# The last 64 keys' scores: from one matmul over a padded block to one matmul per head on half the array

## The chip, the cores and the metric

The kernel runs on one core of a Trainium2 chip. The core has five engines with a queue each, and each works through its own instructions in order: PE (TensorE: matmuls and transposes, which write PSUM), ACT (ScalarE), DVE (VectorE), POOL (GpSimd) and SP, which here only starts DMAs. They wait for each other through semaphores. PSUM has eight banks of 512 float32 columns by 128 partitions. The metric is the device time of one execution in microseconds (us), as the median of several.

## The reference

What is computed, cut to what matters (8 batches, 8 heads, 576 positions, 64 numbers per head; the FFN is 512 to 1024 to 512 wide):

```python
scores = scale * np.matmul(q, k.transpose(0, 1, 3, 2))
kth = np.partition(scores, -top_k, axis=-1)[..., -top_k:-top_k + 1]   # top_k = 32
scores = np.where(scores >= kth, scores, -1000000000.0)
attn = np.exp(scores - np.max(scores, axis=-1, keepdims=True))
attn = attn / (np.sum(attn, axis=-1, keepdims=True) + 1e-09)
attn_out = np.matmul(attn, v)
...
h = np.maximum(x @ w_in, 0.0)             # x: attn_out, heads side by side
conv_out = sum(conv_w[j] * h shifted by j - 1 along the sequence, j = 0, 1, 2)
gate = 1.0 / (1.0 + np.exp(-conv_out))
out = (h * gate) @ w_out
```

## The kernel before

**Tiles.** Two heads make a head pair: head 0 lies on partitions 0 to 63 of the tiles q and k, head 1 on partitions 64 to 127, so that each head's contraction over 64 numbers uses one half of the array's rows. The 576 queries are four blocks of 128 and one of 64. A tile of work is 128 query rows of one head by 576 keys; a block of 128 queries gives two tiles (h = 0 and h = 1, called a pair here), and the block of 64 gives a single one, with the two heads on the two halves of the partitions. There are 128 pairs and 32 singles, 288 tiles in all.

**One tile's way.** Its 576 scores come as 512 "main" keys, one PSUM bank for each head (`s_ps`, L242), and 64 "edge" keys. Head 0's edge is keys 512 to 575. Head 1's keys are stored rotated, so that its edge is its first 64 columns. ACT copies the scores to a row buffer `rows` in SBUF (eight of them, L248 for the main part, L256 for the edges of both heads in one instruction, L250 for a single). DVE finds the 32nd largest by MAX8 over pieces (L266, L286, L288, L315, L319), ACT makes signs (L300, `sides`) and exponentials (L312), POOL multiplies by the signs (L305), DVE masks (L333, tile `e`). PE transposes the 512 main columns of `e` into the bank `pt` (L345), and once a pair the two edges into `mixed` (L358, `tails`); ACT copies them out (L353, L363); PE multiplies with v (L377, L380, into `mixed`) and ACT copies the result out (L387, `xt`). Sums are transposed into a score bank now and then (L398, `norms`).

**The edges before.** The host adds 128 columns to k: head 0's last 64 keys on partitions 0 to 63 in the first 64 columns, head 1's on partitions 64 to 127 in the last 64, and zeros elsewhere. One matmul over all 128 rows of the array (L225, `edge_product`) then gives both heads' edges side by side in 128 columns of the bank `mixed`.

**The FFN.** It runs beside the attention of later batches: 12 matmuls make one unit of the first product in the bank `me` (L454, `e_mm` in the code), ACT applies ReLU to it (L468), POOL and DVE do the convolution and the gate, ACT the tanh (L515), and 12 or 24 further matmuls in the bank `mc` make a block of the output (L611), which ACT copies out (L627).

**Order.** PE, ACT, DVE and POOL run in the order in which `iteration(it)` is written; nothing reorders them. Iteration `it` issues work for nine tiles at different stages, each on its engine: scores of tile it+3, their copy to `rows` for tile it+2, and so on, down to transposes of tile it-5. Within an iteration PE does: the four transposes of tile it-5; FFN matmuls as far as a budget allows (`run_units`); `norms`; `tails`; the edge product of the next pair, if the next tile starts one; the scores, if this tile starts a pair (or is a single); the products with v. ACT does: ReLU and output copies of finished FFN units, `sides`, the copy of a tile's main scores and (for h = 0) of the pair's edges, the copy of `pt`, the copy of the transposed edges (`tailed`), the copies `xt` (`av_out`), the exponentials, tanh. So iterations alternate: in one, PE computes a pair's scores; in the next, ACT copies head 0's scores and the edges, and PE does `tails`, and before the change also the next pair's edge product. A tile in PSUM is waited for as a whole: a matmul into `mixed` waits until ACT has read what an earlier instruction wrote there, in other columns too.

Of the kernel before, what the change touches and what calls it, by code (L numbers as in the profile page):

```python
# [69 lines left out]
def attend_and_feed(ctx: ExitStack, tc: tile.TileContext, q, k, v, weights, out, shared, finish=None):  # L70
# [61 lines left out]
    edge_ps, tail_ps, x_ps = mixed[:, 0:P], mixed[:, P:2 * P], [mixed[:, i * P:(i + 1) * P] for i in (2, 3)]  # L132
    flat = rows.rearrange("p a c -> p (a c)")
# [87 lines left out]
    def edge_product(t):  # L221
        t.edged = True
        row = row_of(t.st.i)
        at = slice(row, row + P)
        nc.tensor.matmul(edge_ps, lhsT=t.pc.nat["q"][:, at], rhs=t.pc.nat["k"][:, S:S + 2 * TAIL], start=True, stop=True)  # L225

    def scores(t):
# [3 lines left out]
        if t.single:  # L231
            for to, n, ps_of in ((0, MAIN, s_ps[0]), (MAIN, TAIL, edge_ps)):
                for h, d in enumerate(rows_of):
                    at = (to + TAIL * h) % S
                    nc.tensor.matmul(ps_of[rows_of[1 - h], 0:n], lhsT=qx[d, row:row + TAIL], rhs=kx[d, at:at + n],  # L235
                                     start=True, stop=True)
        elif t.h == 0:
            at = slice(row, row + P)
            if not t.edged:
                edge_product(t)  # L240
            for h, d in enumerate(rows_of):
                nc.tensor.matmul(s_ps[h], lhsT=qx[d, at], rhs=kx[d, h * TAIL:h * TAIL + MAIN], start=True, stop=True)  # L242

    def evacuate(t):
        t.row = rows[:, t.n % XBUFS]
        x = t.x = t.row[:, 8:S + 8]
        at = TAIL if t.h else 0
        nc.scalar.copy(out=x[:, at:at + MAIN], in_=s_ps[t.h])  # L248
        if t.single:
            nc.scalar.copy(out=x[:, MAIN:S], in_=edge_ps[:, 0:TAIL])  # L250
        elif t.h == 0:
            r = t.n % XBUFS
            if r + 1 < XBUFS:
                first, step = r * (S + 16) + 8 + MAIN, S + 16 - MAIN
                ends = flat[:, first:first + 2 * step].rearrange("p (h c) -> p h c", h=2)[:, :, 0:TAIL]
                nc.scalar.copy(out=ends, in_=edge_ps.rearrange("p (h c) -> p h c", h=2))  # L256
            else:
                nc.scalar.copy(out=x[:, MAIN:S], in_=edge_ps[:, 0:TAIL])
                nc.scalar.copy(out=rows[:, 0, 8:8 + TAIL], in_=edge_ps[:, TAIL:2 * TAIL])
# [422 lines left out]
    for b in range(B):  # L682
        for part, blocks in enumerate(PARTS):
            for g in range(NPAIR):
# [5 lines left out]
                for i in blocks:  # L690
# [4 lines left out]
                    for h in range(1 if single else 2):  # L695
                        t = Box()
                        t.n, t.k, t.h, t.pc, t.st, t.single = len(work), pc.n, h, pc, st, single
                        t.ends, t.edged = single or h == 1, False
# [28 lines left out]
    def run_units(budget, only=None):  # L727
        while budget > 0.0 or (only is not None and only.cur is not None):
            for lane in lanes if only is None else (only,):
# [52 lines left out]
    def iteration(it):  # L782
# [5 lines left out]

        for lane in lanes:
            while lane.finished and lane.finished[0].room():  # L790
                lane.waiting -= 1
                lane.finished.popleft().emit()
# [18 lines left out]
        if tE is not None:  # L811
            transposed(tE)
# [3 lines left out]
        for st in outs:  # L816
            av_out(st)
            if st.final and st.pc.g % 2:
                norm_wait.append((it + NORM_LAG, st.pc))

# [57 lines left out]
        if n + 1 < NT and not (work[n].single or work[n + 1].single or work[n + 1].h):  # L878
            edge_product(work[n + 1])
# [33 lines left out]
    if finish is not None:  # L913
        finish(edge_ps[0:1, 0:1])
# [70 lines left out]
def _layout(inputs):  # L985
# [12 lines left out]
    ends = np.zeros((B, H // 2, 2, D, 2, S - main), k.dtype)  # L998
    for h in range(2):
        ends[:, :, h, :, h] = k[:, h::2, main:].transpose(0, 1, 3, 2)  # L1000
    ends = ends.reshape(B, H // 2, 2 * D, -1)
    tails = np.zeros((B, H // 2, 2, S - main, 2, D), v.dtype)
    for h in range(2):
# [4 lines left out]
        "k": np.concatenate([pairs(k, lambda h: h % 2 == 1), ends], axis=-1),  # L1008
# [30 lines left out]
```

## Time and profile before

| | |
|---|---|
| Median of 3 runs | 1125.31 us (1123.97 to 1125.52) |
| The profiled execution's own time | 1126.22 us |
| Its span (first to last instruction) | 1124.3 us |
| Busy: PE, DVE, ACT, POOL | 1041.0 (93%), 1044.5 (93%), 985.1 (88%), 959.8 (85%) us |
| Chain that ended last | PE 72%, DVE 17%, ACT 8%, DMA 1% |
| Idle of PE ahead of L358 (128 and 32 instructions) | 31.3 and 12.2 us |
| Idle of PE ahead of L225 (256 records of 128 matmuls) | 13.0 us |

A float32 matmul stands in the trace as two passes, each with its own load of weights (LDWEIGHTS, shown as PEld); the counts of L225 and L242 are twice the number of matmuls for that reason. Durations of one instruction overlap with the next one's on every engine, so the distance between two starts says what an instruction takes from its engine. The first 225 us hold the conversion of the FFN's weights and a batch without FFN work; after the last tile, at about 1060 us, only FFN work is left.

### The profile page before, as it was taken

To read this page: it belongs to the slowest core of one execution; us is meant where nothing else is said; L and a number is where in the kernel's file an instruction comes from. 1 tells how busy PE (TensorE), PEld (TensorE's weight loads), DVE (VectorE), ACT (ScalarE), POOL (GpSimd) and SP (SyncE) were. 2 spreads that over 40 slices of the span, in tenths; PEclk is the share of its full clock that TensorE was granted. 3 is DMA by queue.
4 is the path that set the end of the run, shared out by engine and by line. 5 is a ranking of instruction groups with operands and counts; after the bars stand their busy time and mean duration, and the time that the engine had idled before them with its cause. 6 is when DMAs were issued, how large, how long until landed. Compare 5 with 4: busy or idle time off the path is not lost.

```text
span 1124.3 us, 28000 instructions
## 1 busy us (share of the span) xinstructions
PE 1041.0 (93%) x7970; PEld 766.5 (68%) x7970; DVE 1044.5 (93%) x5822; ACT 985.1 (88%) x2504; POOL 959.8 (85%) x1260
## 2 busy tenths in 40 slices
PE   6765589999999999999999999999999999999997
PEld 1443356676777777776777777776777777776885
DVE  6999999999999999999999999999999999999760
ACT  6999989999899998989989898989989898989641
POOL 5989979799898989899898999899898999899800
PEclk9989889999999999999999999999999999999999
DMA  7232231123221331223221321223221331222101
GB/s 254 89 101 79 68 100 56 61 75 115 74 78 51 119 100 54 71 74 123 73 71 60 119 99 54 70 74 126 70 74 60 115 97 60 69 72 82 27 27 44
DMA packets 71157, 92.28 MB, mean 82 GB/s; under 512 B 12848, under 2 KB 37712, under 8 KB 70992
## 3 DMA queue, kind: packets, MB, share of 16 engines
q1 hardware_dynamic: 70992, 90.38, 25.1%
q8 instruction: 66, 1.08, 0.4%
q14 instruction: 99, 0.81, 0.2%
HBM read 80.76 MB, written 9.58 MB: 80 GB/s over the span
## 4 chain that ended last, share of the span: by engine, by line
PE 72%; DVE 17%; ACT 8%; issue 1%; DMA 1%; SPq 0%; ACTq 0%
PE mc L611 15%; PE me L454 14%; PE pt L345 11%; PE mixed L377 11%; PE s L242 9%; DVE cand L266 4%; DVE e L333 3%; DVE z L315 3%; PE mixed L380 2%; PE s L235 2%; PE mixed L225 2%; ACT weights_ps L312 2%; PE mixed L358 2%; PE weights_ps L611 1%; ACT side L300 1%
## 5 line engine op out<-in xcount | busy, mean ns | idle before, releaser
L266 DVE MAX8 cand<-rows 128x8 f32<-128x82 f32 (+1 forms) x2016 | 483.9, 242 | 0.0
L305 POOL TENSOR_TENSOR z<-rows,side 128x579 f32<-128x579 f32 x288 | 347.3, 1206 | 58.5 <-ACT side L300 56.2
L333 DVE SCALAR_TENSOR_TENSOR e<-rows,kth,weights_ps 128x576 f32<-128x576 f32 x288 | 232.2, 806 | 1.5 <-PE mixed L358 0.9
L454 PE MATMUL me<-x_hi,wi 128*128 128x258 f32 (+1 forms) x952 | 229.9, 312 | 1.0 <-ACT g L468 1.0
L312 ACT ACTIVATE weights_ps<-rows,z 128x576 f32<-128x576 f32 x288 | 219.9, 764 | 6.1 <-DVE e L333 4.4
L300 ACT ACTIVATE side<-rows 128x576 bf16<-128x576 f32 x288 | 222.9, 774 | 0.0
L315 DVE MAX8 z<-z 128x8 f32<-128x576 f32 x288 | 214.3, 744 | 1.8 <-POOL z L305 1.8
L345 PEld LDWEIGHTS pt<-ident,e 128*128 128x128 f32 x1152 | 124.5, 144 | 121.5 <-issue 47.6
L611 PE MATMUL mc<-wo,split 128*128 128x512 f32 x732 | 197.1, 402 | 0.0
L353 ACT COPY pT<-pt 128x512 f32<-128x512 f32 x256 | 152.5, 596 | 49.0 <-PE pt L345 48.0
L345 PE MATMUL pt<-ident,e 128*128 128x128 f32 x1152 | 193.6, 292 | 0.2 <-DVE e L333 0.2
L242 PE MATMUL s<-k,q 64*128 64x512 f32 x512 | 178.3, 671 | 3.7 <-ACT rows L248 3.6
L248 ACT COPY rows<-s 128x512 f32<-128x512 f32 x288 | 166.6, 578 | 16.2 <-PE s L242 13.2
L377 PE MATMUL mixed<-pT,vn 128*64 128x128 f32 (+1 forms) x2560 | 166.1, 273 | 2.1 <-ACT pTt L363 2.1
L454 PEld LDWEIGHTS me<-x_hi,wi 128*128 128x128 f32 x952 | 162.9, 191 | 1.7 <-ACT g L468 1.7
L377 PEld LDWEIGHTS mixed<-pT,vn 128*64 128x64 f32 x2560 | 130.7, 139 | 24.1 <-issue 7.2
L611 PEld LDWEIGHTS mc<-wo,split 128*128 128x128 f32 x732 | 128.9, 189 | 20.5 <-issue 0.2
L454 PE MATMUL me<-x_lo,wi 128*128 128x258 f32 (+1 forms) x476 | 142.0, 298 | 0.0
L487 POOL TENSOR_SCALAR t<-g,cr 128x256 f32<-128x256 f32 (+1 forms) x230 | 117.4, 511 | 0.0
L286 DVE MAX8 rows<-cand 128x8 f32<-128x21 f32 x576 | 107.0, 186 | 0.0
L501 POOL TENSOR_TENSOR t<-t,t 128x256 f32<-128x256 f32 (+1 forms) x115 | 92.3, 803 | 9.6
L454 PEld LDWEIGHTS me<-x_lo,wi 128*128 128x128 f32 x476 | 91.1, 191 | 0.0
(133 smaller groups left out, 1788.0 us busy)
## 6 DMA issues: line engine op xcount, KB each, us to landing
k<-in_k_dram SPq DMA_DIRECT2D x64, 352.0 KB
q<-in_q_dram SPq DMA_DIRECT2D x64, 288.0 KB
vn<-in_v_main_dram SPq DMA_DIRECT2D x64, 256.0 KB
out_dram<-o SPq DMA_DIRECT2D x26, 256.0 KB
rb<-row SPq DMA_DIRECT2D x64, 96.0 KB
raw<-in_w_in_dram SPq DMA_DIRECT2D x16, 256.0 KB
vt<-in_v_tail_dram SPq DMA_DIRECT2D x64, 64.0 KB
raw<-in_w_out_dram SPq DMA_DIRECT2D x16, 256.0 KB
```

Of the source, the lines that this page charges most:

```text
L242: nc.tensor.matmul(s_ps[h], lhsT=qx[d, at], rhs=kx[d, h * TAIL:h * TAIL + MAIN], start=True, stop=True)
L248: nc.scalar.copy(out=x[:, at:at + MAIN], in_=s_ps[t.h])
L266: yield lambda c=c, at=at, n=n: nc.vector.max(out=t.cand[:, c:8 * CHUNKS:CHUNKS], in_=t.x[:, at:at + n])
L300: nc.scalar.activation(out=t.side[:, 2:S + 2], in_=t.x, func=AF.Sign, scale=-OVER, bias=t.row[:, 7:8], accum_out=t.cnt)
L305: nc.gpsimd.tensor_tensor(t.z[:, 8:S + 11], t.row[:, 6:S + 9], t.side, ALU.mult)
L312: nc.scalar.activation(out=e_ps, in_=t.x, func=AF.Exp, scale=scale, bias=t.shift)
L315: nc.vector.max(out=t.z[:, 0:8], in_=t.z[:, 10:S + 10])
L333: nc.vector.scalar_tensor_tensor(out=t.e, in0=t.x, scalar=kth[:, t.n:t.n + 1], in1=e_ps, op0=ALU.is_ge, op1=ALU.mult, accum_out=t.pc.sums[ ...
L345: nc.tensor.transpose(tp[:, i * P:(i + 1) * P], t.e[:, o + i * P:o + (i + 1) * P], ident)
L377: nc.tensor.matmul(a[r, 0:w], lhsT=st.pc.vn[:, h, i], rhs=st.pT[:, 1 - h if st.single else h, i, 0:w], start=(i == 0), stop=False)
L454: nc.tensor.matmul(mm[:, 0:w], lhsT=wt, rhs=xx, start=(n == 0), stop=(n == len(ops) - 1))
L611: nc.tensor.matmul(mm[0:m], lhsT=x[:, i], rhs=wo[:, e, f], start=start, stop=stop)
```

## The change

- k has no zero columns any more: 576 columns in place of 704.
- The edges of each head are a matmul of their own with 64 columns over that head's half of the array's rows, issued right ahead of the main scores of the same pair (in singles they now come first as well). Head 0's go to the last 64 columns of `mixed`, head 1's to the last 64 columns of `me`. `edge_product`, and its place an iteration ahead, are gone.
- ACT copies them with two instructions of 64 columns, and these (or a single's one) are the first of ACT's iteration, ahead of ReLU, output copies and `sides`.
- ACT's copy of `pt` (`transposed`) moves behind `tailed` and `av_out`.
- An argument of `run_units` that nothing used is gone.

```diff
 
     s_ps = [bank(f"s{h}") for h in range(2)]
     e_mm, mixed = bank("me"), bank("mixed")
-    edge_ps, tail_ps, x_ps = mixed[:, 0:P], mixed[:, P:2 * P], [mixed[:, i * P:(i + 1) * P] for i in (2, 3)]
-    flat = rows.rearrange("p a c -> p (a c)")
+    edge_ps = [x[:, BANK - TAIL:BANK] for x in (mixed, e_mm)]
+    tail_ps, x_ps = mixed[:, 0:P], [mixed[:, i * P:(i + 1) * P] for i in (1, 2)]
 
     scratch = []
 
...
         nc.sync.dma_start(out=vn, in_=v_main[pc.b, pc.g])
         nc.sync.dma_start(out=vt, in_=v_tail[pc.b, pc.g])
 
-    def edge_product(t):
-        t.edged = True
-        row = row_of(t.st.i)
-        at = slice(row, row + P)
-        nc.tensor.matmul(edge_ps, lhsT=t.pc.nat["q"][:, at], rhs=t.pc.nat["k"][:, S:S + 2 * TAIL], start=True, stop=True)
-
     def scores(t):
         kx, qx = t.pc.nat["k"], t.pc.nat["q"]
         row = row_of(t.st.i)
         rows_of = [slice(h * D, (h + 1) * D) for h in range(2)]
         if t.single:
-            for to, n, ps_of in ((0, MAIN, s_ps[0]), (MAIN, TAIL, edge_ps)):
+            for to, n, ps_of in ((MAIN, TAIL, edge_ps[0]), (0, MAIN, s_ps[0])):
                 for h, d in enumerate(rows_of):
                     at = (to + TAIL * h) % S
                     nc.tensor.matmul(ps_of[rows_of[1 - h], 0:n], lhsT=qx[d, row:row + TAIL], rhs=kx[d, at:at + n],
                                      start=True, stop=True)
         elif t.h == 0:
             at = slice(row, row + P)
-            if not t.edged:
-                edge_product(t)
-            for h, d in enumerate(rows_of):
-                nc.tensor.matmul(s_ps[h], lhsT=qx[d, at], rhs=kx[d, h * TAIL:h * TAIL + MAIN], start=True, stop=True)
+            for ps_of, keys in ((edge_ps, [(MAIN, S), (0, TAIL)]), (s_ps, [(0, MAIN), (TAIL, S)])):
+                for h, d in enumerate(rows_of):
+                    nc.tensor.matmul(ps_of[h], lhsT=qx[d, at], rhs=kx[d, keys[h][0]:keys[h][1]], start=True, stop=True)
 
     def evacuate(t):
+        at = TAIL if t.h else 0
+        nc.scalar.copy(out=t.x[:, at:at + MAIN], in_=s_ps[t.h])
+
+    def evacuate_edges(t):
         t.row = rows[:, t.n % XBUFS]
-        x = t.x = t.row[:, 8:S + 8]
-        at = TAIL if t.h else 0
-        nc.scalar.copy(out=x[:, at:at + MAIN], in_=s_ps[t.h])
-        if t.single:
-            nc.scalar.copy(out=x[:, MAIN:S], in_=edge_ps[:, 0:TAIL])
-        elif t.h == 0:
-            r = t.n % XBUFS
-            if r + 1 < XBUFS:
-                first, step = r * (S + 16) + 8 + MAIN, S + 16 - MAIN
-                ends = flat[:, first:first + 2 * step].rearrange("p (h c) -> p h c", h=2)[:, :, 0:TAIL]
-                nc.scalar.copy(out=ends, in_=edge_ps.rearrange("p (h c) -> p h c", h=2))
-            else:
-                nc.scalar.copy(out=x[:, MAIN:S], in_=edge_ps[:, 0:TAIL])
-                nc.scalar.copy(out=rows[:, 0, 8:8 + TAIL], in_=edge_ps[:, TAIL:2 * TAIL])
+        t.x = t.row[:, 8:S + 8]
+        if t.h == 0:
+            if not t.single:
+                nc.scalar.copy(out=rows[:, (t.n + 1) % XBUFS, 8:8 + TAIL], in_=edge_ps[1])
+            nc.scalar.copy(out=t.x[:, MAIN:S], in_=edge_ps[0])
 
     def chunk_ops(t):
         t.cand = att.tile([P, 8 * CHUNKS], F32, name="cand", bufs=4)
...
                     for h in range(1 if single else 2):
                         t = Box()
                         t.n, t.k, t.h, t.pc, t.st, t.single = len(work), pc.n, h, pc, st, single
-                        t.ends, t.edged = single or h == 1, False
+                        t.ends = single or h == 1
                         pc.n += 1
                         work.append(t)
                 pcs.append(pc)
...
         pre, tA, tB, tC = (tiles.get(i) for i in (it + 2, it, it - 1, it - 2))
         tX, tD, tE = tiles.get(it - 3), tiles.get(it - 4), tiles.get(it - 5)
 
+        if pre is not None:
+            evacuate_edges(pre)
         for lane in lanes:
             while lane.finished and lane.finished[0].room():
                 lane.waiting -= 1
...
             sides(tC)
         if pre is not None:
             evacuate(pre)
-        if tE is not None:
-            transposed(tE)
         while tail_next:
             tailed(tail_next.pop())
         outs, out_next = out_next, []
...
             av_out(st)
             if st.final and st.pc.g % 2:
                 norm_wait.append((it + NORM_LAG, st.pc))
+        if tE is not None:
+            transposed(tE)
 
         if exact:
             a_ops, b_ops = [], list(exact_ops(tB)) if tB is not None else []
...
         rec_next = recs + rec_next
         if both:
             tails(tE)
-        if n + 1 < NT and not (work[n].single or work[n + 1].single or work[n + 1].h):
-            edge_product(work[n + 1])
         if n < NT:
             scores(tiles[n])
         for st in avs:
...
         for it in range(-3, NT + 6):
             iteration(it)
     if finish is not None:
-        finish(edge_ps[0:1, 0:1])
+        finish(edge_ps[0][0:1, 0:1])
     while expands or contracts or any(x.waiting for x in lanes) or pool_tasks or tanh_next or tanh_now or gates:
         it += 1
         iteration(it)
...
                  for h in range(H)]
         return np.stack(heads, axis=1).reshape(B, H // 2, 2 * D, S)
 
-    ends = np.zeros((B, H // 2, 2, D, 2, S - main), k.dtype)
-    for h in range(2):
-        ends[:, :, h, :, h] = k[:, h::2, main:].transpose(0, 1, 3, 2)
-    ends = ends.reshape(B, H // 2, 2 * D, -1)
     tails = np.zeros((B, H // 2, 2, S - main, 2, D), v.dtype)
     for h in range(2):
         tails[:, :, h, :, h] = v[:, h::2, main:]
 
     arrays = {
         "q": pairs(q, lambda h: False),
-        "k": np.concatenate([pairs(k, lambda h: h % 2 == 1), ends], axis=-1),
+        "k": pairs(k, lambda h: h % 2 == 1),
         "v_main": v[:, :, :main].reshape(B, H // 2, 2, main // P, P, D).transpose(0, 1, 4, 2, 3, 5),
         "v_tail": tails.reshape(B, H // 2, 2 * (S - main), 2, D),
         "w_in": inputs["moe_w_in"],
```

In the changed kernel the new numbers of the lines spoken of are: L235 for a pair's edges and main scores (L229 in singles), L239 for the copy of main scores, L246 and L247 for the copies of head 1's and head 0's edges, L288 `sides`, L300 the exponentials, L333 the transposes, L341 the copy of `pt`, L346 `tails`, L351 and L375 the copies of the transposed edges and of `xt`, L365 and L368 the products with v, L386 `norms`, L442 and L599 the FFN's matmuls, L456 the ReLU, L503 tanh.

PE, from FFN matmuls through two iterations, in the kernel before. `s_121` and `s_122` are the two score banks, `k,q` the two tiles of a head pair, 64x128 the shape of an output.

```order
L611 MATMUL mc<-wo,split 128x512 x3
L358 MATMUL mixed<-ident,e_10289 128x128
L225 MATMUL mixed<-k,q 128x128
L242 MATMUL s_121<-k,q 128x512
L242 MATMUL s_122<-k,q 128x512
L345 MATMUL pt<-ident,e_10399 128x128 x4
L398 MATMUL s_121<-ident,rec 6x128
L358 MATMUL mixed<-ident,e_10399 64x128
L225 MATMUL mixed<-k,q 128x128
L377 MATMUL mixed<-pT,vn 64x128 x8
L380 MATMUL mixed<-pTt,vt 64x128 x2
```

The same place after the change:

```order
L599 MATMUL mc<-wo,split 128x512 x3
L346 MATMUL mixed<-ident,e_10445 128x128
L235 MATMUL mixed<-k,q 128x64
L235 MATMUL me<-k,q 128x64
L235 MATMUL s_121<-k,q 128x512
L235 MATMUL s_122<-k,q 128x512
L333 MATMUL pt<-ident,e_10557 128x128 x4
L386 MATMUL s_121<-ident,rec 6x128
L346 MATMUL mixed<-ident,e_10557 64x128
L365 MATMUL mixed<-pT,vn 64x128 x8
L368 MATMUL mixed<-pTt,vt 64x128 x2
```

The 128-column edge product between `tails` and the products with v is gone, and two matmuls of 64 columns stand ahead of the main scores, one of them into `me`.

ACT, one iteration that copies head 0's scores and the one after it, before. `side_109` and `side_113` are the two sign tiles, `weights_ps` holds the exponentials and a tanh.

```order
L300 ACTIVATE side_109,cnt<-rows 128x576
L248 COPY rows<-s_121 128x512
L256 COPY rows<-mixed 128x2x64
L353 COPY pT<-pt 128x512
L312 ACTIVATE weights_ps<-rows,z 128x576
L515 ACTIVATE weights_ps<-t_4539,cw 128x256
L468 ACTIVATE g_4161<-me 128x258
L300 ACTIVATE side_113,cnt<-rows 128x576
L248 COPY rows<-s_122 128x512
L353 COPY pT<-pt 128x512
L363 COPY pTt<-mixed 128x128
L387 COPY xt_4750<-mixed 128x128
```

The same two iterations after the change:

```order
L246 COPY rows<-me 128x64
L247 COPY rows<-mixed 128x64
L288 ACTIVATE side_109,cnt<-rows 128x576
L239 COPY rows<-s_121 128x512
L341 COPY pT<-pt 128x512
L300 ACTIVATE weights_ps<-rows,z 128x576
L503 ACTIVATE weights_ps<-t_4611,cw 128x256
L456 ACTIVATE g_4229<-me 128x258
L288 ACTIVATE side_113,cnt<-rows 128x576
L239 COPY rows<-s_122 128x512
L351 COPY pTt<-mixed 128x128
L375 COPY xt_4823<-mixed 128x128
```

The edges' copies moved from behind the main copy to the head of the iteration and are two; in the second iteration the copy of `pt` (L341, the next row after these) moved from ahead of the two copies out of `mixed` to behind them.

More of the change, by code (lines that the diff above doesn't have):

```diff
@@ L725, in start, with run_units @@
             ffn(pc.b, pc.part)
-    def run_units(budget, only=None):
-        while budget > 0.0 or (only is not None and only.cur is not None):
-            for lane in lanes if only is None else (only,):
+    def run_units(budget):
+        while budget > 0.0:
+            for lane in lanes:
                 if lane.cur is None:
```

## The prediction

> **What bounds the kernel now.** I read the stages first, then PE's waits inside the longest one, then who runs ahead of whom. The stages (us, busy us of PE, PEld, DVE, ACT, POOL with counts, granted clock, DMA share, GB/s):
>
> ```profile
> 225.00:1060.00 835.00, 815.73 (x6575) 614.51 (x6574) 804.40 (x4590) 760.55 (x1932) 764.88 (x986) 1.00 0.26 81
> 0.00:225.00 225.00, 169.21 (x1088) 103.40 (x1088) 212.63 (x1183) 203.19 (x528) 187.99 (x266) 0.95 0.31 101
> 1060.00:1124.00 64.00, 56.06 (x310) 48.59 (x308) 27.51 (x53) 21.39 (x46) 6.99 (x10) 0.97 0.10 34
> ```
>
> In the first 225 us PE idles 55.8 us and DVE 12.4: DVE sets the pace, and a PE wait there is worth nothing. From 225 to 1060 PE is busy 815.7 of 835 us (97.7%), DVE 804.4 (96.3%). Which of the two leads? DVE finished masking a tile (566.70 + 0.80), and PE began its transposes 3.0 us later:
>
> ```profile
> 566.70 0.80 DVE L333 SCALAR_TENSOR_TENSOR e<-rows,kth,weights_ps 128x576 f32<-128x576 f32 x1
> 570.49 0.66 PE L345 MATMUL pt<-ident,e 128*128 128x128 f32 x4
> ```
>
> So PE is the late one, its own queue of work is the bound, and time is gained only from PE's work or PE's waits. Its waits in that stage, all of them (total us, times, longest):
>
> ```profile
> PE mixed L358 <- ACT pTt L363: 6.9, 8, 1.8
> PE mixed L358 <- ACT xt L387: 5.4, 5, 1.5
> PE s L398 <- ACT rows L248: 4.9, 6, 0.9
> PE me L454 <- ACT g L468: 1.0, 3, 0.3
> PE mixed L358 <- ACT rows L256: 0.4, 2, 0.2
> ```
>
> 18.6 us, 1.7% of the time: no rearrangement of waits can give more. Nearly all are `tails` or `norms` standing behind an ACT copy. The waits of the other two engines follow from PE's lateness for the most part:
>
> ```profile
> ACT pT L353 <- PE pt L345: 44.7, 78, 2.0
> DVE hot L319 <- ACT weights_ps L515: 13.0, 25, 1.0
> ```
>
> **PE's work: the edge product goes, two half-array matmuls come.** What the old one takes from PE is read from starts:
>
> ```profile
> 565.68 0.27 PE L358 MATMUL mixed<-ident,e 128*128 128x128 f32 x1
> 565.79 0.39 PE L225 MATMUL mixed<-k,q 128*128 128x128 f32 x2
> L225 PE MATMUL mixed<-k,q 128*128 128x128 f32 x200 | 38.7, 275 | 0.0
> ```
>
> The edge product's two passes start 0.11 us after `tails` and, with 0.39 us for two of 0.275, 0.11 apart: 0.22 us of PE for one, in a full-array stretch, so that no change of array mode goes with it. There are 100 in the stage (200 records), 22 us.
>
> The new ones stand in a stretch that already works on halves of the array:
>
> ```profile
> 562.80 1.13 PE L242 MATMUL s<-k,q 64*128 64x512 f32 x4
> 563.86 0.66 PE L345 MATMUL pt<-ident,e 128*128 128x128 f32 x4
> 562.80 0.30 PEld L242 LDWEIGHTS s<-k,q 64*128 64x128 f32 x4 [0.36 <-issue]
> 565.68 0.30 PEld L225 LDWEIGHTS mixed<-k,q 128*128 128x128 f32 x2
> 364.90 0.28 PE L235 MATMUL mixed<-k,q 64*64 64x64 f32 x4
> ```
>
> The main scores hold PE for 1.06 us (563.86 - 562.80). Two full loads in sequence take 0.30 us, 0.11 apart; the four half loads of the main scores take 0.30 together, so the halves load at the same time. The 64-column passes of a single (L235) take 0.28 us for four, in two steps 0.06 apart. With 128 columns of weights a pass of 0.055 us is shorter than the load of 0.11, so the loads set the pace: each half needs two more, 2 x 0.11 = 0.22 us ahead of the main scores. Net: 0.22 - 0.22 = 0. From below, loads that hid wholly would leave the passes, 0.11 us (a gain of 0.11, 14 us over 128 pairs); from above, halves that loaded one after the other would cost 0.44 (a loss of 0.22, 28 us). I take 0, since L242 is the same kind of matmul with the same weights. In singles only the order within the group changes.
>
> The Trainium skill ("TensorE: Matmul & The Clock Gate", on packing small matmuls, "The mechanism") says that a weight load overlaps a running matmul "only when row_grp differs", that is, only when it goes to other rows of the array. The four loads of L242 are over 0.30 us after the start, while each half's first pass, some 0.5 us of the 1.06 for both, still streams: the trace does not bear the rule out here.
>
> **PE's waits.** ACT's copy of `pt` moves behind the copies out of `mixed`. Two places of a few that repeat with each two batches:
>
> ```profile
> 540.35 0.59 ACT L350 COPY pT<-pt 128x512 f32<-128x512 f32 x1
> 540.82 0.28 ACT L363 COPY pTt<-mixed 128x128 f32<-128x128 f32 x1
> 540.98 0.24 ACT L387 COPY xt<-mixed 128x64 f32<-128x64 f32 x1
> 541.27 0.30 PE L358 MATMUL mixed<-ident,e 128*64 128x128 f32 x1 [1.50 <-ACT xt L387]
> 547.34 0.59 ACT L353 COPY pT<-pt 128x512 f32<-128x512 f32 x1 [0.85 <-PE pt L345]
> 547.82 0.39 ACT L387 COPY xt<-mixed 128x128 f32<-128x128 f32 x2
> 548.26 0.33 PE L358 MATMUL mixed<-ident,e 128*128 128x128 f32 x1 [0.96 <-ACT xt L387]
> ```
>
> At 541 the `pt` copy keeps ACT 0.47 us (540.82 - 540.35) ahead of what PE waits for; without it 1.50 becomes 1.03. The eight waits for L363 (the copy of transposed edges) shorten alike: 8 x 0.47 = 3.8 us. At 548 ACT had stood 0.85 us itself before that copy, so both `xt` copies fit into its own wait and the whole 0.96 goes. Of the five waits for L387 I count two of each kind and one more of the first: 3 x 0.47 + 2 x 0.96 = 3.3 us. The waits for L256 go (0.4), since the edges' copies are first now. Against it: `norms` waits for head 0's main copy, which now has the edges' copies ahead of it. A 64-column copy takes 0.10 us from ACT, a 128-column one 0.16:
>
> ```profile
> 561.31 0.27 ACT L363 COPY pTt<-mixed 128x128 f32<-128x128 f32 x1
> 561.47 0.23 ACT L387 COPY xt<-mixed 128x64 f32<-128x64 f32 x1
> 561.57 0.77 ACT L312 ACTIVATE weights_ps<-rows,z 128x576 f32<-128x576 f32 x1
> ```
>
> 6 x 0.2 = 1.2 us lost. Sum of the waits: 3.8 + 3.3 + 0.4 - 1.2 = 6.3 us gained.
>
> **ACT's head of the iteration.** The two copies cost 0.20 in place of 0.16, 0.04 us for each of 128 pairs, 5 us of ACT; ACT's idle time (74 us in the stage) covers it. More serious: everything in ACT's iteration now stands behind the edges.
>
> ```profile
> 562.79 0.76 ACT L300 ACTIVATE side<-rows 128x576 bf16<-128x576 f32 x1
> 563.96 0.59 ACT L248 COPY rows<-s 128x512 f32<-128x512 f32 x1 [0.31 <-PE s L242]
> 564.44 0.27 ACT L256 COPY rows<-mixed 128x128 f32<-128x128 f32 x1
> 564.60 0.60 ACT L353 COPY pT<-pt 128x512 f32<-128x512 f32 x1
> 569.51 0.40 ACT L468 ACTIVATE g<-me 128x258 f32<-128x258 f32 x1
> 570.90 0.37 PE L454 MATMUL me<-x_hi,wi 128*128 128x258 f32 x1
> ```
>
> PE began the scores at 562.80 and ACT its iteration at 562.79. Edges would be there 0.22 + 0.22 us later (loads, and the 0.22 that a 64-column pass takes end to end), 563.24; ACT stands 0.45 us, copies until 563.44, starts `sides` 0.65 us late. But it waited 0.31 us for the main scores at 563.96 anyway, and L256's 0.16 is gone: the `pt` copy comes at 564.78, 0.18 late. Where ReLU comes first (569.51; scores from 569.43) it ends at 570.48 instead of 569.91, still before PE wants `me` at 570.90. POOL waits behind `sides`, DVE behind both, and they have the 3.0 us of lead. I take 0 for the time, and price the other case below.
>
> **The start.** k's tile is 64 KB smaller:
>
> ```profile
> 4.02 6.02 DMA raw<-in_w_in_dram
> k<-in_k_dram SPq DMA_DIRECT2D x64, 352.0 KB
> ```
>
> The chain that ended last begins with loads of FFN weights, queued behind two k and two q. Ahead of its end, 6.02 us after its issue, land those four (1280 KB), a small load and itself (280 KB); 128 KB of 1560 is 0.5 us of 6.02 at most. I take 0.3. Later the DMA engines are a quarter busy.
>
> **Sum.** 0 (work) - 6.3 (waits) + 0 (ACT) - 0.3 = -6.6 us. The profiled execution took 1126.22 us, so 1119.6 for it; the median shown is 0.9 us lower, 1125.31, so 1118.7, forecast 1119.
>
> **Rivals.**
> *ScalarE's stall reaches PE (slower).* Place: the copy of `me` at the head of ACT's iteration. In the stage ACT waited for main scores 29 times (12.0 us), so it is as early as at 562.8 in at least those, and each would start `sides` and ReLU about 0.6 us late, 0.2 to 0.4 of it not recovered in the same iteration:
>
> ```profile
> ACT rows L248 <- PE s L242: 12.0, 29, 0.9
> ```
>
> It decides if DVE's lead of 3.0 us is used up or a ReLU ends after PE reaches the FFN (0.4 us of room above). Price: 29 x 0.4 = 11.6, less the 6.6: 1130. For it: DVE is only 1.4% less busy than PE and already waits for ACT. Against: those are the iterations in which PE is late.
> *The loads don't hide (slower).* If a load waits for the pass before it on its own half, each of two passes adds 0.055 us: 0.11 x 128 = 14 us, 1119 + 14 = 1133. This is what the rule of the Trainium skill quoted above comes to here. For it: no row has a 64-column pass with 128 columns of weights. Against: L242's loads.
> *No change.* DVE's busy time is untouched, and its waits in the stage leave little room; if PE's freed time only moves into waits for DVE or POOL, 1125. Against: the 3.0 us.
> *More gain.* In 78 iterations ACT waits for `pt`; the copies behind it, 0.32 us, now fall into that wait, up to 25 us of ACT, and exponentials and tanh come sooner for DVE. That helps only where DVE is the late one, from 130 to 300 us above all: about 8 us more, 1111.
>
> **How the numbers follow.** Forecast 0.50 (its own range 1115 to 1122.5), no change 0.20, ScalarE's stall 0.14, loads 0.06, more gain 0.10. A measurement of this kernel can tell about 0.2% (2.3 us) from no change. Faster by over that: 0.48 + 0.10 = 0.58; within: 0.02 + 0.20 = 0.22; slower: 0.20. The low end, 1109, lies past the larger gain and takes in the lower bound of the matmuls (1125 - 14) by itself; the high end, 1131, lies just past the stall's 1130 and leaves the loads' 1133 out.
>
> **What would show it.** From the first start of L235 to the next transposes it should be 1.28 us where L242 took 1.06, and 1.39 if loads don't hide. PE's waits for `mixed` in the same stage should fall from 12.7 to about 5 us, those of `norms` rise from 4.9 to 6. ACT should show a wait at L246 of some 0.4 us in about half the pairs, and PE none at the ReLU beyond today's 1.0. If PE's idle time in the stage does not fall, or DVE's masking ends less than 1 us before PE's transposes, the forecast is wrong.

## The result, and the profile after

The change made the kernel slower, by 0.8%:

| | median, us | runs, us | ratio to before, 95% interval |
|---|---|---|---|
| before | 1124.82 | 4, 1123.97 to 1125.52 | |
| after | 1134.14 | 4, 1133.77 to 1134.52 | 1.0083 [1.0066, 1.0101] |
| forecast | 1119 | range 1109 to 1131 | |

The profiled execution of after took 1133.77 us, with a span of 1131.9. Its stages, with the columns as before; the long one ends 7 us later, so that it holds about the same work:

```profile
0.00:225.00 225.00, 161.12 (x1149) 100.55 (x1149) 213.93 (x1190) 205.53 (x560) 189.26 (x268) 0.91 0.31 97
225.00:1067.00 842.00, 814.13 (x6770) 600.21 (x6769) 802.41 (x4581) 761.42 (x2022) 764.36 (x985) 1.00 0.24 76
1067.00:1131.90 64.90, 56.74 (x313) 49.13 (x311) 26.98 (x53) 21.28 (x48) 6.20 (x9) 0.97 0.10 34
```

The long stage grew from 835 to 842 us, while PE, DVE and POOL are about as busy as before (814.1, 802.4, 764.4 us; 815.7, 804.4, 764.9 before). So the time went into waits, not into work: PE's listed waits are 27.1 us in the stage, 18.8 before. The main ones, from 225 to 1060 us:

```profile
PE s L386 <- ACT rows L239: 9.5, 10, 1.5
PE mixed L235 <- ACT xt L375: 7.3, 11, 1.2
PE mixed L346 <- ACT xt L375: 4.8, 8, 1.3
PE mixed L346 <- ACT pTt L351: 2.1, 2, 1.7
```

The waits of `tails` fell, from 12.7 us to 6.9. But `norms` (L386) now waits 9.5 us instead of 4.9, and the scores, which before never waited for the bank `mixed`, wait 7.3. Not all of that is new: 4.0 of it stand at four places from 330 to 351 us, where before a pair's scores took 1.92 to 2.41 us instead of 1.06, standing for their second bank in the middle (listed under the load of weights). ACT's own waits:

```profile
ACT rows L247 <- PE mixed L368: 29.9, 21, 2.2
ACT rows L246 <- PE me L235: 26.7, 48, 1.0
```

Before, ACT stood mainly 44.7 us ahead of the `pt` copy. Now it stands at the edges' copies at the head of its iteration. L246 is the pairs' copy, which the prediction named. L247 behind L368 is the singles' copy, and nothing in the prediction has it. Its longest wait, on ACT, and what it did to DVE:

```profile
367.19 0.21 ACT L247 COPY rows<-mixed 128x64 f32<-128x64 f32 x1 [2.23 <-PE mixed L368]
367.30 0.45 ACT L456 ACTIVATE g<-me 128x322 f32<-128x322 f32 x1
367.63 0.78 ACT L288 ACTIVATE side<-rows 128x576 bf16<-128x576 f32 x1
370.31 0.23 DVE L307 SCALAR_TENSOR_TENSOR hot<-weights_ps,cnt,z 128x10 f32<-128x10 f32 x1 [1.05 <-ACT weights_ps L300]
```

And what PE did meanwhile:

```profile
364.65 0.33 PE L229 MATMUL mixed<-k,q 64*64 64x64 f32 x4
364.82 1.03 PE L229 MATMUL s<-k,q 64*64 64x512 f32 x4
365.78 1.09 PE L365 MATMUL mixed<-pT,vn 128*64 128x128 f32 x16
366.70 0.39 PE L368 MATMUL mixed<-pTt,vt 128*64 128x128 f32 x4
```

The single's edge scores began at 364.65 and took 0.33 us. But behind the single's scores PE issues products with v (L365, L368), which write other columns of the same bank `mixed`, and the bank is waited for as a whole. So a copy that is ready at about 365.0 stands until 367.19, and everything in ACT's iteration behind it (ReLU, `sides`, the copies, the exponentials) stands too. In the chain that ended last PE's share fell from 72% to 49%; ACT's rose from 8% to 13% and DVE's from 17% to 32%:

```profile
PE 49%; DVE 32%; ACT 13%; POOL 2%; issue 2%; DMA 1%; SPq 0%; ACTq 0%; POOLq 0%; DVEq 0%
```

DVE's rise does not belong to the singles' copy, since DVE has 34% in run e2 below, where that copy is back in its place. But it says that PE is the last in less of the long stage than before: from 499 to 556 us, for one, the chain does not touch PE.

### The profile page after: what moved, and what is told of

It is laid out like the page before. It is cut to its first block, busy times and chain, and to the rows that moved or that the text cites. A ratio compares the mean times of both kernels' runs of the same rounds, so it can differ in the third digit from the quotient of the medians.

```text
span 1131.9 us, 28673 instructions
## 1 busy us (share of the span) xinstructions
PE 1032.0 (91%) x8226; PEld 749.9 (66%) x8226; DVE 1043.3 (92%) x5822; ACT 988.2 (87%) x2628; POOL 959.8 (85%) x1260
## 4 chain that ended last, share of the span: by engine, by line
PE 49%; DVE 32%; ACT 13%; POOL 2%; issue 2%; DMA 1%; SPq 0%; ACTq 0%; POOLq 0%; DVEq 0%
PE mc L599 12%; PE me L442 10%; DVE cand L254 8%; DVE e L321 7%; PE mixed L365 7%; PE pt L333 6%; DVE z L303 5%; PE s L235 5%; DVE cand L276 3%; ACT side L288 3%; PE mixed L235 2%; ACT weights_ps L300 2%; DVE rows L274 2%; DVE g L511 2%; DVE hot L307 1%
## 5 line engine op out<-in xcount | busy, mean ns | idle before, releaser
L442 PE MATMUL me<-x_hi,wi 128*128 128x258 f32 (+1 forms) x952 | 228.7, 311 | 0.8 <-ACT rows L246 0.3
L300 ACT ACTIVATE weights_ps<-rows,z 128x576 f32<-128x576 f32 x288 | 221.3, 768 | 6.6 <-POOL z L293 2.7
L288 ACT ACTIVATE side<-rows 128x576 bf16<-128x576 f32 x288 | 226.4, 786 | 0.0
L333 PEld LDWEIGHTS pt<-ident,e 128*128 128x128 f32 x1152 | 124.7, 144 | 135.8 <-ACT rows L247 28.3
L599 PE MATMUL mc<-wo,split 128*128 128x512 f32 x732 | 198.5, 403 | 2.5 <-POOL split L574 1.4
L333 PE MATMUL pt<-ident,e 128*128 128x128 f32 x1152 | 194.9, 293 | 4.2 <-DVE e L321 3.9
L365 PE MATMUL mixed<-pT,vn 128*64 128x128 f32 (+1 forms) x2560 | 167.9, 275 | 2.2 <-ACT pTt L351 2.2
L239 ACT COPY rows<-s 128x512 f32<-128x512 f32 x288 | 169.1, 587 | 0.0
L365 PEld LDWEIGHTS mixed<-pT,vn 128*64 128x64 f32 x2560 | 132.4, 141 | 49.8 <-issue 41.8
L442 PEld LDWEIGHTS me<-x_hi,wi 128*128 128x128 f32 x952 | 161.7, 190 | 3.9 <-ACT g L456 2.2
L341 ACT COPY pT<-pt 128x512 f32<-128x512 f32 x256 | 155.0, 605 | 4.8 <-PE pt L333 1.1
L235 PE MATMUL s<-k,q 64*128 64x512 f32 x512 | 156.4, 659 | 2.4 <-ACT rows L239 1.9
L599 PEld LDWEIGHTS mc<-wo,split 128*128 128x128 f32 x732 | 128.9, 189 | 24.4 <-POOL split L578 2.4
L442 PE MATMUL me<-x_lo,wi 128*128 128x258 f32 (+1 forms) x476 | 141.4, 297 | 0.0
L235 PE MATMUL mixed<-k,q 64*128 64x64 f32 x256 | 57.5, 306 | 45.7 <-ACT xt L375 34.0
```

Of the source, the lines that this page charges most:

```text
L235: nc.tensor.matmul(ps_of[h], lhsT=qx[d, at], rhs=kx[d, keys[h][0]:keys[h][1]], start=True, stop=True)
L239: nc.scalar.copy(out=t.x[:, at:at + MAIN], in_=s_ps[t.h])
L288: nc.scalar.activation(out=t.side[:, 2:S + 2], in_=t.x, func=AF.Sign, scale=-OVER, bias=t.row[:, 7:8], accum_out=t.cnt)
L300: nc.scalar.activation(out=e_ps, in_=t.x, func=AF.Exp, scale=scale, bias=t.shift)
L333: nc.tensor.transpose(tp[:, i * P:(i + 1) * P], t.e[:, o + i * P:o + (i + 1) * P], ident)
L365: nc.tensor.matmul(a[r, 0:w], lhsT=st.pc.vn[:, h, i], rhs=st.pT[:, 1 - h if st.single else h, i, 0:w], start=(i == 0), stop=False)
```

## The experiments

Twelve kernels, all compared with the kernel before on the same chip (its median there was 1124.6 to 1125.4 us). All of them compute everything. Waits are those from 225 to 1060 us. The names of the edits: "pt late" is the copy of `pt` behind the copies out of `mixed`; "pairs first" and "singles first" are the edges' copies at the head of ACT's iteration, for pairs and for singles; "split edges" is one matmul per head in two banks, made right ahead of the main scores.

| kernel | edges | pt late | pairs first | singles first | median, us | ratio, 95% interval |
|---|---|---|---|---|---|---|
| after | split | yes | yes | yes | 1134.14 | 1.0083 [1.0066, 1.0101] |
| e1 | split | yes | no | no | 1172.02 | 1.0416 [1.0397, 1.0435] |
| e2 | split | yes | yes | no | 1121.47 | 0.9965 [0.9954, 0.9977] |
| e4 | product | yes | no | no | 1115.37 | 0.9913 [0.9896, 0.9930] |
| e5 | product | yes | yes | yes | 1127.64 | 1.0019 [1.0009, 1.0029] |
| e6 | product | yes | yes | no | 1115.20 | 0.9915 [0.9898, 0.9931] |
| e9 | split | yes | behind `sides` | no | 1137.66 | 1.0122 [1.0105, 1.0138] |
| e12 | split | no | yes | no | 1138.50 | 1.0130 [1.0113, 1.0146] |
| e15 | product, late | yes | yes | no | 1119.25 | 0.9948 [0.9931, 0.9964] |

### The edges' copies back behind the main copy (e1), and the singles' copy alone (e2)

On after; e2 has the lines with `single`, e1 does it for pairs as well (`place` only picks the tile's row buffer):

```diff
         if pre is not None:
-            evacuate_edges(pre)
+            place(pre)
+            if not pre.single:
+                evacuate_edges(pre)
...
             evacuate(pre)
+            if pre.single:
+                evacuate_edges(pre)
```

> The changed kernel, but ScalarE's copies of the edges (pairs and singles) stand behind the copy of the main scores again, still two instructions of 64 columns; the matmuls stay as changed. Theory A (ScalarE stands at the head of its iteration, most of all in singles, where the copy waits for the products with v that write the same bank): the time falls from 1134 to 1126 or less, the waits of the edges' copies (27 and 33 us in the stage from 225 us on) go to under 10, and norms' waits fall from 9.5 to about 5 us. Theory B (the scores now stand behind the xt copy, since their first matmul writes into mixed): the time stays at 1131 to 1135, and PE's wait at the first edge matmul stays at 7 us.

> The changed kernel, but only the singles' edge copy stands behind the main copy again; pairs keep theirs first. Theory A: most of the loss is in the singles' copies (30 us of ScalarE waiting for the products with v), so 1134 falls to about 1128. Theory B: 1132 to 1135.

e1 took 1172.02 us. One line of its PE waits says why:

```profile
PE me L444 <- ACT rows L248: 40.8, 78, 1.3
```

Head 1's edges lie in the FFN's bank `me`. With their copy late, the FFN's first matmul behind the scores waits for it, 78 times. So for pairs the early copy is no choice of its own: the second bank forces it. This run couldn't test the early copies, since it opened a worse wait.

e2 took 1121.47, 12.7 us less than after. The single's copy alone turned the change from a gain into a loss. Its waits, PE's first:

```profile
PE mixed L235 <- ACT xt L377: 7.3, 11, 1.3
PE s L388 <- ACT rows L243: 7.1, 6, 1.2
PE mixed L348 <- ACT xt L377: 2.5, 2, 1.2
PE mixed L348 <- ACT pTt L353: 2.4, 2, 1.7
```

```profile
ACT rows L248 <- PE me L235: 35.9, 58, 1.1
ACT rows L249 <- PE mixed L370: 4.1, 7, 0.6
```

ACT's wait at the single's copy fell from 29.9 to 4.1 us, while the one for the pairs' is even longer than in after (35.9 us against 26.7): that one is not what made after slow. Behind the main copy it comes when the products with v are done or nearly so. The way to the end can be followed at one single, in after:

```profile
400.00 0.21 ACT L247 COPY rows<-mixed 128x64 f32<-128x64 f32 x1 [0.82 <-PE mixed L368]
401.35 0.22 ACT L375 COPY xt<-mixed 128x64 f32<-128x64 f32 x1
401.63 0.33 PE L346 MATMUL mixed<-ident,e 128*128 128x128 f32 x1 [0.38 <-ACT xt L375]
```

and at the same single in e2, where nothing on ACT waits, `sides` starts straight behind the tanh, and the two copies follow the main one:

```profile
395.47 0.53 ACT L505 ACTIVATE weights_ps<-t,cw 128x320 f32<-128x320 f32 x1
395.94 0.76 ACT L290 ACTIVATE side<-rows 128x576 bf16<-128x576 f32 x1
397.16 0.21 ACT L249 COPY rows<-mixed 128x64 f32<-128x64 f32 x1
397.26 0.22 ACT L377 COPY xt<-mixed 128x64 f32<-128x64 f32 x1
```

ACT stands 0.82 us, so `xt` leaves `mixed` late, and `tails`, which has to write there, waits. Start by start, after falls 0.54 us behind e2 at this one `tails`, and 0.29 at `norms` 3.7 us later. From 382 to 638 us, two batches, seven such steps of 0.24 to 0.56 us (three at `tails`, two at `norms`, two at the FFN's next unit) make up nearly all of the 2.8 us by which after falls back. The FFN's steps are those of the ReLU (L456), which stands behind the singles' copy too. Such a wait is listed at the load of weights, here from 366.9 to 368.2 us in after:

```profile
PEld me L442 <- ACT g L456: 0.4, 1, 0.4
```

DVE waits longer for the exponentials too (31.0 us in the stage, 23.4 in e2), but the steps are not its doing: PE begins a tile's transposes a median of 2.7 us after DVE has masked it, and none of PE's listed waits in the stage is for DVE.

### The pt copy alone (e4), and the new order with the old product (e5, e6)

e4 is before with only the `pt` copy moved; e5 moves all edges' copies first as well; e6 is e5 with the singles' copy behind the main one:

```diff
-        if tE is not None:
-            transposed(tE)
         while tail_next:
             tailed(tail_next.pop())
...
             av_out(st)
+        if tE is not None:
+            transposed(tE)
```

> The kernel before, with nothing changed but the place of ScalarE's copy of pt, which moves behind the copies out of mixed. By the prediction's working this alone is worth 7.1 us of waits (3.8 + 3.3), so 1118. If waits that go come back elsewhere: 1122 to 1126. If the move itself costs: above 1127.

> The kernel before with its edge product over the padded keys an iteration ahead, but with the whole new order on ScalarE: the edges' copies (one instruction for a pair) first in the iteration, pt's copy behind the copies out of mixed. The edges of a pair are ready an iteration earlier here, so ScalarE never stands for them. Theory A (standing at the head): pairs cost nothing, singles still wait for the products with v; 1120 to 1126. Theory B: no edge matmul stands ahead of the scores, so 1118 to 1122. If the new order itself is the loss, 1130 or more.

> The kernel before with its edge product, pt's copy moved, and the edges' copy first in ScalarE's iteration for pairs alone; a single's stays behind the main copy. Theory A (a single's copy, put first, waits for the products with v): against the run with all copies first (1127.6) the 36 us of ScalarE's waits for them go and the time falls to 1113 to 1117, no slower than the pt move alone (1115.4), since a pair's edges are ready long before here. If copies first cost in pairs too: 1119 to 1127.

e4, at 1115.37, is 9.7 us faster than before. PE's waits in it, with 12.7 us for `mixed` become 5.0:

```profile
PE s L398 <- ACT rows L248: 6.8, 6, 1.5
PE mixed L358 <- ACT pTt L363: 3.0, 2, 1.7
PE mixed L358 <- ACT xt L387: 2.0, 2, 1.0
```

Not all of the gain lies in the long stage. Compared by the starts of DVE's maskings, e4's profiled execution (10.7 us shorter than that of before) is 3.1 us ahead at 227 us and 10.5 at the last tile, so 7.4 us come in the long stage. Of the 3.1 us, 2.5 come between 134 and 150 us, where DVE had stood for the exponentials, which follow the copies on ACT. Its waits there in before, and in e4:

```profile
DVE hot L319 <- ACT weights_ps L312: 2.2, 3, 1.6
```

```profile
DVE hot L319 <- ACT weights_ps L312: 0.2, 1, 0.2
```

e5 loses all of it and more, at 1127.64, though its matmuls are those of before, and e6 has it back, at 1115.20. So the price of the singles' copy, 12.4 us here and 12.7 from e2 to after, does not hang on the split edges. Its wait on ACT in e5, and in e6:

```profile
ACT rows L252 <- PE mixed L382: 27.1, 21, 2.2
```

```profile
ACT rows L255 <- PE mixed L385: 3.9, 8, 1.2
```

From e4 to e6 only the pairs' copy moves to the head: 0.2 us, which is nothing. There the product was made an iteration earlier, and ACT hardly stands for the bank (10.2 us in the stage, 6.2 of them for the product itself).

### The products with v kept from behind a single's scores (e14a, e14b)

On e5 (e14a) and, as control, on e6 (e14b):

```diff
-        avs = [st for st in av_next if not crowded or it > st.at]
+        avs = [st for st in av_next if not (crowded or (n < NT and work[n].single)) or it > st.at]
```

> The kernel with the old edge product and all copies first (1127.6), but in a single's iteration PE makes no product with v behind the single's scores; it comes an iteration later. Theory A (the single's copy, at the head, waits for those products because they write the same bank): that wait (27 us in the stage) falls under 8 us although the copy stays first, and the time to 1115 to 1120. If it is the copy's place itself: 1125 or more.

> Control for the run before this one: the same later product with v, in the kernel whose singles' copy stands behind the main copy (1115.2). It shows what the later product costs by itself: 1114 to 1119 under every theory.

With the copies first 1131.34 us (1.0060 [1.0044, 1.0077]), in the control 1129.94 (1.0042 [1.0027, 1.0056]). The time of e14a missed what was expected by far, and so did its control's. But the difference between the two is what counts: the singles' copy first costs 1.4 us, inside the intervals, where it cost 12.4. The copy's wait for products with v is gone, and what it still waits for is its own scores, 13.2 us in e14a:

```profile
ACT rows L252 <- PE mixed L235: 13.2, 14, 1.1
```

So it is the products with v behind the single's scores that make the early copy dear. One reservation stays: both runs are slow for another reason, which may hide a part of the copy's price. The edit itself cost the control 14.7 us. In both runs the pairs' copy now waits for the products, which follow an iteration later. In e14b:

```profile
ACT rows L261 <- PE mixed L385: 19.3, 16, 1.9
```

That looks like the same mechanism, moved from singles to pairs. That this wait makes the 14.7 us was not tested.

### What split edges cost: without the pt move (e12), and the old product made late (e15)

e12 is e2 with the copy of `pt` in its old place. e15 is e6 without the early product, which is then made right ahead of the pair's scores, as the split edges are:

```diff
-        if n + 1 < NT and not (work[n].single or work[n + 1].single or work[n + 1].h):
-            edge_product(work[n + 1])
         if n < NT:
             scores(tiles[n])
```

> The changed kernel with the singles' copy back and pt's copy back in its old place: what is left is the matmuls on half the array and the pairs' copies first. If the parts add up: 1121.5 + 9.7 = 1131. If the pt move only pays for something that the split edges need: 1136 or more. If the two share a gain: 1126 or less.

> The kernel with the old edge product, pt's copy moved and pairs' copies first (1115.2), but the product of a pair is issued right ahead of its main scores instead of an iteration ahead: still one full-array matmul into mixed, no half array, nothing in the FFN's bank. Theory B+C (what is left, 6 us, comes from edges that are made just in time: PE's scores stand behind the xt copy in mixed, ScalarE stands for the edges): 1120 to 1124, with a PE wait at L225 of 5 us or more in the stage. Theory D (it comes from the half-array matmuls or from sharing the FFN's bank): 1114 to 1117.

e12 took 1138.50, so with split edges the `pt` move is worth 17.0 us, not 9.7. The longest of its PE waits:

```profile
PE mixed L235 <- ACT xt L377: 14.0, 16, 1.4
```

It is new with the change: the scores' first matmul writes to `mixed` and waits for `xt`, 14.0 us. In before the scores wrote to their own banks only, and the edge product came right behind `tails`, which had already waited for the bank.

e15 shows the same with the old matmul: 4.0 us over e6, at 1119.25, with these waits of PE and of ACT:

```profile
PE mixed L225 <- ACT xt L392: 5.6, 11, 1.0
```

```profile
ACT rows L261 <- PE mixed L225: 24.3, 48, 0.9
```

So 4.0 of the 6.3 us between e6 and e2 come from making a pair's edges just in time. Two waits come with it: PE's scores wait behind `xt`, and ACT's iteration waits for the edges. How much each of them carries wasn't separated, and the traces can't tell, since the profiled execution of e6, at 1118.31 us, was the slowest of its four.

The other 2.2 us come with the rest of the change together: the half arrays, the second bank and a pair's second copy, a single's edges ahead of its main scores, the smaller k. In pairs they are not PE's work: from the start of `tails` over edges and scores to the next transposes PE takes 1.48 us in e15, and 1.48 in after with split edges, where a place without edges takes 1.26. A place in before, and one in e15:

```profile
296.00 0.27 PE L358 MATMUL mixed<-ident,e 128*128 128x128 f32 x1
296.20 1.13 PE L242 MATMUL s<-k,q 64*128 64x512 f32 x4
297.26 0.44 PE L345 MATMUL pt<-ident,e 128*128 128x128 f32 x2
```

```profile
670.12 0.27 PE L363 MATMUL mixed<-ident,e 128*128 128x128 f32 x1
670.23 0.39 PE L225 MATMUL mixed<-k,q 128*128 128x128 f32 x2
670.54 1.13 PE L242 MATMUL s<-k,q 64*128 64x512 f32 x4
671.60 0.66 PE L350 MATMUL pt<-ident,e 128*128 128x128 f32 x4
```

What the 2.2 us are is open.

### Three other orders of ACT's queue (e9, e13, e11)

e9 is e2 with the pairs' copies behind `sides`, just ahead of the main copy. e13 is e2 with the copies out of `mixed` (`tailed`, `av_out`) ahead of the main copy (a single's edges go with the main copy), and e11 the same on e4:

```diff
             sides(tC)
-        if pre is not None:
-            evacuate(pre)
         while tail_next:
             tailed(tail_next.pop())
...
+        if pre is not None:
+            evacuate(pre)
         if tE is not None:
             transposed(tE)
```

> The changed kernel with the singles' copy back and the pairs' copies behind sides and ahead of the main copy. Theory C (the 6 us that are left between 1121.5 and 1115.4 are ScalarE standing for a pair's edges, 36 us in the stage): that wait falls below 10 us and the time to 1116 to 1118. Theory B (they are PE's wait for the xt copy at the first edge matmul, 7.3 us in the stage): 1120 to 1123, with that wait still 6 us or more. If the FFN's first matmul waits for the later copy out of its bank, as with all copies back: above 1124.

> The changed kernel with the singles' copy back and ScalarE's copies out of mixed (transposed edges and xt) ahead of the main copy, so about 0.6 us earlier. Theory B: PE's wait for xt at the first edge matmul falls from 7.3 to under 2 us and the time from 1121.5 to 1116 to 1118. Theory C: no change in time beyond 2 us.

> The kernel before with pt's copy moved (1115.4), and the copies out of mixed put still earlier, ahead of the main copy. If PE's remaining waits for mixed (5.0 us in the stage) are still time to be had: 1111 to 1113. If the same happens as in the changed kernel (the waits for mixed shrink, ScalarE stands for the products with v and norms waits longer): 1114 to 1117.

e9 took 1137.66 us, 16.2 more than e2, most of it for the reason of e1: the FFN waits for its bank 29 times.

```profile
PE me L444 <- ACT rows L248: 14.0, 29, 1.0
```

e13 took 1121.98 (0.9977 [0.9968, 0.9987]), no gain over e2. The wait of the scores for `xt` halved, but other waits took its place, on PE and on ACT:

```profile
PE mixed L235 <- ACT xt L377: 3.5, 6, 0.9
PE s L388 <- ACT rows L243: 9.5, 10, 1.5
```

```profile
ACT pTt L353 <- PE mixed L370: 12.1, 24, 0.7
ACT xt L377 <- PE mixed L370: 10.6, 22, 0.8
```

e11 took 1118.61 (0.9936 [0.9919, 0.9952]), 3.2 us more than e4, with ACT standing 18.7 and 16.9 us at the same two copies. The `pt` move takes one copy out of the way of what PE and DVE wait for. Going one place further makes ACT stand for products that are not finished. Of all versions e4 and e6 are the fastest. They beat both kernels, by 0.9% before and 1.7% after, and e4 is a move of two lines.

## Why the prediction was wrong

The measured parts, each the difference of two medians, from before (1125.1 in these runs) to after:

| step | from, to | us |
|---|---|---|
| the `pt` copy late | before, e4 | -9.7 |
| pairs' copies first | e4, e6 | -0.2 |
| edges made right ahead of the scores | e6, e15 | +4.0 |
| the rest: half arrays, two banks and copies, singles' edges first, smaller k | e15, e2 | +2.2 |
| singles' copy first | e2, after | +12.7 |
| sum | | +9.0 |

The parts depend on their order: with split edges the `pt` move is worth 17.0.

**What bounds the kernel: right in the main.** PE is the late one at the transposes of the long stage, and the loss came as PE waits. But two things were read too simply. DVE is only just behind: the chain of after runs through it for stretches of the long stage, and in the first 225 us, where a PE wait was said to be worth nothing, the `pt` move still gained, through DVE's waits for ACT. And "all of them" was not all of PE's waits. The list has idle time behind a modelled end of a matmul, so that at 401.63 it has 0.38 us where the starts moved 0.54, and waits at a load stand under PEld. Over the last 240 tiles the starts moved 10.2 us from e2 to after, while PE's listed waits rose by 5.3. Still, the sign that the prediction had named as its refutation, that PE's idle time in the stage does not fall, is what came.

**PE's work, 0: right.** From the first start of L235 to the next transposes it is 1.283 us in all 100 pairs of the long stage, as forecast:

```profile
564.85 0.32 PE L235 MATMUL mixed<-k,q 64*128 64x64 f32 x1
565.12 1.08 PE L235 MATMUL s<-k,q 64*128 64x512 f32 x4
566.13 0.66 PE L333 MATMUL pt<-ident,e 128*128 128x128 f32 x4
```

What they add ahead of the scores, 0.22 us, is what the old product had taken between `tails` and the products with v (0.42 us from start to start with it, 0.20 without). The rival of loads that don't hide wanted 1.39 and falls. The Trainium skill ("TensorE: Matmul & The Clock Gate", "The mechanism") lets a weight load overlap a running matmul only on other rows of the array; the 1.283 us here do not agree with it.

**PE's waits, -6.3: the `pt` move right, its price for others missed.** 7.1 us had been counted for the `pt` move from single places, and 7.4 came in the long stage of e4. The other part of its 9.7 lies in the first 225 us. Missed was that the edges, put ahead of the scores, bring a wait of their own: the scores' first matmul for `xt`, 7.3 us in after, of which 4.0 replace a wait of the scores of before. The prediction worked out which copies `tails` waits for and did not ask who else would now write to `mixed`. It also took 1.2 us for `norms`, because of the edges' copies ahead of the main one. Its wait rose by 4.6. It is 6.8 in e4, where no edges' copy has moved, so that 1.9 of the rise come with the `pt` move, and 9.5 in after against 7.1 in e2 says that about half of the rise belongs to the singles.

**ACT's head of the iteration, taken as 0: the step that failed.** For pairs the stall came as described (48 times, 26.7 us at L246). It cost nothing where the product is early, and at most 4.0 us, together with the scores' wait, where it is late. But of singles the prediction said only that "the order within the group changes". It costed the stall from PE's edge matmuls, not from the last writer that the copy waits for. In pairs these are the same instruction, or the copy comes an iteration later; in singles the products with v lie between. That cost 12.7 us and alone decided the sign: e2, without it, took 1121.5, inside the forecast's own range. Even that would have been partly luck, since the `pt` move gained 2.6 us more than counted, and 6.2 us for edges made late, two banks and the rest had not been foreseen.

**The start, -0.3: not shown.** The first masking is 0.3 us earlier in after, but 0.4 in e4, where k still has its zero columns.

**The rivals.** "ScalarE's stall reaches PE" had the direction and, at 1130, nearly the size, but its place was wrong: the pairs it counted are not where most of the time went. The path was the singles' copy, then `xt` and the main copies behind it for `tails` and `norms`, and the ReLU, which it had named, for a smaller part. Its chance of 0.14 was too small because the room was read at one pair. "More gain" was right in its mechanism and place for a small part: in e4 exponentials came sooner for DVE, which gave 2.5 us between 134 and 150 us. "No change" falls, since the time moved both ways, by the parts above.

## What to carry to other kernels

An instruction at the head of an in-order queue must be costed from the last writer of what it waits for, for each kind of iteration (pairs and singles here), not from the instruction that makes its data. Sharing a buffer that is waited for as a whole, such as a PSUM bank, binds the order of everything that writes there: ask who waits for it now, and who waits next when something late is put in. Where a change has several parts, time each part by itself, since here a two-line move was worth 0.9% and was hidden under a loss.

## What the runs showed of the hardware

Matmuls on the two halves of the array load their weights beside each other: the four edge matmul passes and the main scores behind them hold PE for 1.283 us, and the edges' passes start 0.16 and 0.11 us apart.

One full-array product of 128 columns takes 0.22 us, behind other full-array work as well as right ahead of half-array scores: between `tails` and the products with v the starts lie 0.42 us apart with it and 0.20 without, and from `tails` to the transposes 1.48 with it (e15) and 1.26 without (before). Counted from its own start to the transposes, 1.37 us against 1.06 for the scores alone, it seems to cost 0.31. But the instruction ahead is then nearer: from `tails` to the next start it is 0.11 us where the product follows and 0.20 where half-array scores do. So the passage from a full-array matmul to one on half the array (half its rows in the scores, half its columns in the products with v) costs about 0.09 us in these rows, once, on whichever side of the product it falls.
